# An attention and feed-forward kernel: another order of attention blocks, weights converted earlier through three raw buffers, and the activations' cast on ScalarE

## The chip, the cores and the metric

The kernel runs on one core of a Trainium2 chip. A core has five engines that work side by side, each through its own instructions in order: TensorE (PE in the profile; its weight loads are PEld) multiplies matrices, VectorE (DVE) and GpSimd (POOL) do elementwise work, ScalarE (ACT) does functions and copies, and SyncE (SP) issues most transfers. The metric is the device time of one execution in microseconds, the median of several.

## The reference

Attention over 2 batches of 8 heads, 768 positions and 64 numbers a head, where each query sees the first 8 keys and the 96 up to itself, then two feed-forward layers over the 1536 tokens, all in float32.

```python
scores = scale * np.matmul(q, k.transpose(0, 1, 3, 2))
is_global = pos[None, :] < int(n_global)            # 8
is_local = (rel >= 0) & (rel < int(n_local))        # 96
scores = scores + bias[None, :, :, :]               # -slope of the head * distance
scores = np.where(is_global | is_local, scores, -1000000000.0)
a = np.exp(scores - np.max(scores, axis=-1, keepdims=True))
x = np.matmul(a / (np.sum(a, axis=-1, keepdims=True) + 1e-09), v)   # then tokens x 512
h = x @ w_in                                        # 512 -> 2048
x = (np.maximum(h, 0.0) + np.log1p(np.exp(-np.abs(h)))) @ w_out     # 2048 -> 512
h = x @ w2_in
out = (h * np.clip(h + 3.0, 0.0, 6.0) / 6.0) @ w2_out
```

## The kernel before

**Attention.** The 1536 tokens are 12 blocks of 128, six for each batch, taken in the order 0 to 11. The heads of a block are taken in two quads of four, so there are 24 quads; quad k belongs to block k // 2. A quad has three steps: `s`, its scores (line 445), with a reduction on VectorE (L451), exponentials on ScalarE (L456), and VectorE's reciprocals (L341, L342) that GpSimd multiplies in (L344, tile `pm`); `t`, the transposes of the probabilities (L477, copied by ScalarE in L479 to `pT`); and `v`, the product with the values (L495, `px`). A block sees the slot of its own 128 keys and that of the block before. The first block of a batch has no block before: its two quads have one slot (128 keys) where others have two (256). I call them cheap quads below. `load_block` loads a block's `qT`, `kT` and `V` when the scores of the block ahead of it are taken.

**Feed-forward layers.** Each float32 matrix is split in a high and a low part, and each product is made of three matmuls (L179). A layer's 2048 hidden numbers are 16 chunks of 128. A weight *unit* is one chunk of `w_in` (u = 0) or `w_out` (u = 1), 512 KB of 64-bit words: `unit_load` issues its transfer on SP's queue into a buffer `raw` (two of them at that time), `unit_convert` makes the two parts: ScalarE takes the magnitude (L121), GpSimd clips it (L124), VectorE puts the bits together (L125, L128, L129), `cast` makes the high part (`w0`, `w2`; L98 on GpSimd while `in_first` holds, else L100 on ScalarE), and VectorE the low one (`w1`, `w3`; L134). `w3_1` is the low part of `w_out` of chunk 1, `wa` the work tile, and `raw3_1` the raw words of unit 1 of chunk 3. An activation `g` is computed by `split_g` and split into `gh` (a `cast`, like that of the weights) and `gl` (L171). Names with an f at the end (`ghf`, `accf`, `hf`) are those of the first phase.

**The program's order.** A lead of five steps (`LEAD`) takes the first quads; behind each step `LEAD_UNITS` says how many units are converted. Then `run` goes through 18 items: six groups of 256 tokens, each with three pairs of chunks. An item has two halves of 24 matmuls: h (`hf`, the products with `w_in`) and o (`accf`, those with `w_out`). They are interleaved as h0, h1, h2, o0, h3, o1, h4, o2 and so on. A half also carries one quad's `s` and `v` at its start and two transposes inside; behind it `HALF_UNITS` units are converted (one, where the table has ended). Attention ends with the items' first dozen; then its buffers are given to more weight slots and raw buffers (`grow`). When the 18 items are done, `in_first` falls, and 78 items with matmuls 512 wide follow, with little but matmuls on the path. A scheduler orders each engine's instructions from this program.

```python
            rest = between()
            for z, call in enumerate(calls):
                for f in rest.get(z, ()):
                    f()
                self.ordered(call)
            self.weight_step(HALF_UNITS[min(self.halves, len(HALF_UNITS) - 1)])
```

Of the kernel before, what the change touches and what calls it, by code (L numbers as in the profile page):

```python
# [29 lines left out]
H_AHEAD = 2  # L30
LEAD_UNITS = (0, 1, 1, 1, 1)
HALF_UNITS = (1, 1, 2, 1, 1, 1, 1)
WARM, FILL = 12, (6, 4, 2, 0, 0)
# [15 lines left out]
class Layers:  # L49
# [6 lines left out]
    def __init__(self, ctx, tc, weights, xsh, xsl, out):  # L56
        self.ctx, self.tc, self.nc = ctx, tc, tc.nc
        self.weights, self.xsh, self.xsl, self.out = weights, xsh, xsl, out
        self.pool("mp", 2)
# [10 lines left out]
        self.free, self.h_tags, self.acc_tags, self.wr = [], [], [], []  # L70
        self.n_h, self.halves, self.in_first = 0, 0, True
        self.grow(0, FIRST_SLOTS, 2, 2)
# [22 lines left out]
    def cast(self, out, in_):  # L95

        if self.in_first:
            self.nc.gpsimd.tensor_scalar(out=out, in0=in_, scalar1=1.0, scalar2=0.0, op0=ALU.mult, op1=ALU.add)  # L98
        else:
            self.nc.scalar.copy(out, in_)  # L100

    def unit_load(self, x):
        j, u = self.order[x]
        layer, f = divmod(j, NCH)
        raw = self.wr[x % len(self.wr)].tile([P, CW, 2], I32, tag="raw", name=f"raw{j}_{u}")
        self.nc.sync.dma_start(out=raw.rearrange("p c t -> p (c t)"), in_=self.weights[2 * layer + u][f])
        self.raws[x] = raw
# [28 lines left out]
    def weight_step(self, m):  # L136
        total = 4 * NCH
        for _ in range(m):
            x = self.done
            if x >= total or (self.order[x][1] == 0 and not self.free):  # L140
                return
            while self.loaded <= min(x + 2 * len(self.wr) - 1, total - 1):
                self.unit_load(self.loaded)
                self.loaded += 1
            self.unit_convert(x)
            self.done += 1

    def split_g(self, layer, hf, n):
# [6 lines left out]
        if layer == 0:  # L155
            t2 = self.tp.tile([P, 512], F32, tag="t", name=f"t2{n}")
            nc.scalar.activation(t1, hf, AF.Abs)  # L157
            nc.scalar.activation(t1, t1, AF.Exp, scale=-1.0)
            if self.in_first:
                nc.gpsimd.tensor_scalar(out=t2, in0=t1, scalar1=1.0, scalar2=1.0, op0=ALU.mult, op1=ALU.add)  # L160
            else:
                nc.scalar.add(t2, t1, 1.0)
            nc.scalar.activation(t3, t2, AF.Ln)
            nc.vector.scalar_tensor_tensor(out=t2, in0=t2, scalar=-1.0, in1=t1, op0=ALU.add, op1=ALU.subtract)  # L164
            nc.vector.scalar_tensor_tensor(out=t3, in0=hf, scalar=0.0, in1=t3, op0=ALU.max, op1=ALU.add)  # L165
            nc.vector.tensor_tensor(out=t3, in0=t3, in1=t2, op=ALU.subtract)
# [64 lines left out]
    def item(self, layer, ph, G, s):  # L231
# [17 lines left out]
        for m in range(4):  # L249
# [35 lines left out]
    def run(self, att=None, spare_step=lambda: None):  # L285
# [61 lines left out]
def fast_path(tc, ident, nf, q, k, qt, kt, v, weights, out, flag):  # L347


    with ExitStack() as ctx, ExitStack() as actx:  # L350
        nc = tc.nc
        xsh, xsl = x_tiles(ctx, tc)
        layers = Layers(ctx, tc, weights, xsh, xsl, out)
        tp = layers.tp
        ap2 = actx.enter_context(tc.tile_pool(name="ap2", bufs=2))
        ap_v = actx.enter_context(tc.tile_pool(name="ap_v", bufs=3))
# [5 lines left out]
        ps_x = actx.enter_context(tc.tile_pool(name="ps_x", bufs=1, space=PSUM))  # L362
        kT = ap1.tile([P, KC, 3, P], F32, name="kT")
        gk = ap1.tile([P, KC, MAX_GLOBAL], F32, name="gk")
        qT, V, px = {}, {}, {}
        zeros = ap1.tile([P, 512], BF16, name="zeros")
        nc.vector.memset(zeros, 0.0)

        def load_block(n):
            qT[n] = ap2.tile([P, KC, P], F32, tag="qT", name=f"qT{n}")  # L370
            V[n] = [ap_v.tile([P, DM], F32, tag="V", name=f"V{n}")]
            for cs in (slice(0, 1), slice(1, KC)) if n == 0 else (slice(0, KC),):
                nc.sync.dma_start(out=qT[n][:, cs], in_=qt[n][:, cs])
                nc.sync.dma_start(out=kT[:, cs, n % 3, :], in_=kt[n][:, cs])
# [391 lines left out]
```

## Time and profile before

| what | value |
|---|---|
| median of three runs | 686.46 us (685.08 to 688.02) |
| profiled execution | 685.12 us, its span 683.3 us |
| TensorE busy | 634.4 us (93% of the span), mean granted clock 0.972 |
| VectorE, ScalarE, GpSimd busy | 437.8, 357.2 and 166.4 us |

The span runs from the first to the last instruction that the profiler saw; what the execution takes beyond it (1.8 us) lies around it. [...] A busy share is a mean over stages: the stage with the attention and the first phase of the layers (up to about 235 us) looks unlike the one behind it.

### The profile page before, as it was taken

How to read it: one execution, taken by the hardware profiler on the slowest of the kernel's cores; microseconds unless marked ns; L12 is line 12 of the kernel's file. 1: busy time of each engine (PE TensorE's matmuls, PEld its weight loads, DVE VectorE, ACT ScalarE, POOL GpSimd, SP SyncE). 2: the span in 40 equal slices, each digit the busy share in tenths (PEclk: the TensorE clock that was granted, in tenths of full speed). 3: DMA queues.
4: the chain of work that ended last, by engine and by line, in shares of the span. 5: the costliest groups of instructions: out<-in, count | busy, mean ns of one | idle time of the engine just before them, and what ended most of it. 6: DMA issues, size and time to landing. Idle time of an engine off the chain costs nothing.

```text
span 683.3 us, 9612 instructions
## 1 busy us (share of the span) xinstructions
PE 634.4 (93%) x3481; PEld 522.1 (76%) x3481; DVE 437.8 (64%) x894; ACT 357.2 (52%) x749; POOL 166.4 (24%) x237
## 2 busy tenths in 40 slices
PE   8764876999997999999999999999999999999996
PEld 4553766888996988787888888888888788888884
DVE  6868345555399999999998999322752424324243
ACT  6945434776553477677677765233667222222221
POOL 4884433433255442234320021000100000000000
PEclk9988888999999999999999999999999999999998
DMA  7433323121023224142320123100265000001011
GB/s 231 143 113 116 109 66 116 39 67 55 33 93 124 94 92 147 70 154 93 123 94 31 62 64 121 63 0 1 78 197 157 1 1 0 1 0 62 0 63 66
DMA packets 24936, 53.66 MB, mean 79 GB/s; under 512 B 2480, under 2 KB 8880, under 8 KB 24880
## 3 DMA queue, kind: packets, MB, share of 16 engines
q1 hardware_dynamic: 24880, 52.96, 23.9%
q8 instruction: 29, 0.48, 0.3%
q14 instruction: 27, 0.22, 0.1%
HBM read 49.81 MB, written 3.15 MB: 77 GB/s over the span
## 4 chain that ended last, share of the span: by engine, by line
PE 65%; DVE 21%; ACT 5%; POOL 3%; issue 3%; DMA 1%; POOLq 0%; DVEq 0%; SPq 0%; ACTq 0%
PE acc L179 27%; PE h L179 26%; PE hf L179 4%; DVE wa L128 4%; PE accf L179 3%; DVE w L134 3%; DVE wa L129 3%; ACT pm L456 2%; POOL pm L344 2%; PE ptp L477 2%; PE s L445 2%; DVE wa L125 2%; PE px L495 1%; DVE pm L451 1%; DVE t2f L164 1%
## 5 line engine op out<-in xcount | busy, mean ns | idle before, releaser
L179 PE MATMUL h<-xsh,w 128*128 128x512 f32 x624 | 170.5, 396 | 1.9 <-DVE t3f L165 1.6
L179 PEld LDWEIGHTS h<-xsh,w 128*128 128x128 f32 x624 | 116.7, 188 | 30.6 <-DVE t3f L165 1.8
L179 PE MATMUL acc<-w,gh 128*128 128x512 f32 x384 | 120.6, 395 | 0.0
L124 POOL TENSOR_SCALAR wa<-wa 128x512 f32<-128x512 f32 x64 | 66.4, 1041 | 219.5 <-ACT wa L121 218.0
L169 DVE SCALAR_TENSOR_TENSOR t<-t,h 128x512 f32<-128x512 f32 x48 | 32.9, 686 | 98.2 <-ACT t L168 98.1
L168 ACT ACTIVATE t<-h,three 128x512 f32<-128x512 f32 x48 | 33.0, 687 | 107.2 <-PE h L179 107.0
L179 PE MATMUL h<-xsl,w 128*128 128x512 f32 x312 | 86.7, 395 | 0.0
L179 PE MATMUL accf<-ghf,w 128*128 128x256 f32 x288 | 66.8, 312 | 20.5 <-DVE w L134 20.4
L179 PEld LDWEIGHTS acc<-w,gh 128*128 128x128 f32 x384 | 72.0, 188 | 17.5
L171 DVE TENSOR_TENSOR gl<-t,gh 128x512 fp32r<-128x512 f32 x78 | 55.4, 710 | 46.3 <-ACT gh L100 46.1
L179 PE MATMUL acc<-gh,w 128*128 128x512 f32 x240 | 78.2, 396 | 1.3 <-DVE part L264 1.3
L100 ACT CAST gh<-t 128x512 fp32r<-128x512 f32 x78 | 48.3, 619 | 58.2 <-PE acc L179 25.6
L179 PE MATMUL acc<-w,gl 128*128 128x512 f32 x192 | 76.1, 396 | 0.1
L179 PEld LDWEIGHTS accf<-ghf,w 128*128 128x128 f32 x288 | 52.5, 211 | 23.2 <-DVE w L134 21.7
L179 PEld LDWEIGHTS h<-xsl,w 128*128 128x128 f32 x312 | 58.5, 188 | 14.0
L344 POOL TENSOR_SCALAR pm<-pm,rs 128x256 f32<-128x256 f32 (+1 forms) x96 | 52.5, 565 | 46.9 <-DVE rs L342 35.1
L134 DVE TENSOR_TENSOR w<-wa,w 128x512 fp32r<-128x512 f32 x64 | 46.5, 730 | 16.2 <-POOL w L98 8.9
L179 PEld LDWEIGHTS acc<-gh,w 128*128 128x128 f32 x240 | 45.1, 188 | 12.9 <-ACT t L157 1.7
L121 ACT ACTIVATE wa<-raw 128x512 f32<-128x512 f32 x64 | 42.5, 673 | 22.8 <-DVE w L134 14.4
L456 ACT ACTIVATE pm<-pm,nm 128x256 f32<-128x256 f32 (+1 forms) x96 | 46.2, 484 | 14.8 <-DVE nm L451 14.7
L179 PE MATMUL hf<-xsh,w 128*128 128x256 f32 x288 | 45.7, 290 | 7.9 <-DVE w L134 7.9
L451 DVE CUSTOM_DVE_ANT_0 pm<-s,bias 128x256 f32<-128x256 f32 (+1 forms) x96 | 33.4, 397 | 28.9 <-PE s L445 27.2
(90 smaller groups left out, 1008.3 us busy)
## 6 DMA issues: line engine op xcount, KB each, us to landing
raw<-in_w1i SPq DMA_DIRECT2D x16, 512.0 KB, 3.3
raw<-in_w1o SPq DMA_DIRECT2D x16, 512.0 KB, 3.3
raw<-in_w2i SPq DMA_DIRECT2D x16, 512.0 KB, 3.2
raw<-in_w2o SPq DMA_DIRECT2D x16, 512.0 KB, 3.3
V<-in_v SPq DMA_DIRECT2D x12, 256.0 KB, 2.9
chk<-in_q SPq DMA_DIRECT2D x12, 256.0 KB, 3.4
chk<-in_k SPq DMA_DIRECT2D x12, 256.0 KB, 2.8
out_x<-part SPq DMA_DIRECT2D x12, 256.0 KB, 2.1
```

The costliest lines, as they stand in the source:

```text
L100: self.nc.scalar.copy(out, in_)
L121: first = nc.scalar.activation(a, raw.bitcast(F32)[:, :, 1], AF.Abs)
L124: nc.gpsimd.tensor_scalar(out=a, in0=a, scalar1=W_HI, scalar2=W_LO, op0=ALU.min, op1=ALU.max)
L128: nc.vector.scalar_tensor_tensor(out=ai, in0=hi, scalar=-2 ** 30, in1=ai, op0=ALU.bitwise_and, op1=ALU.bitwise_or)
L134: nc.vector.tensor_tensor(out=wl, in0=a, in1=r32(wh), op=ALU.subtract)
L168: nc.scalar.activation(t1, hf, AF.Relu, bias=self.three[:, 0:1])
L169: nc.vector.scalar_tensor_tensor(out=t3, in0=t1, scalar=6.0, in1=hf, op0=ALU.min, op1=ALU.mult)
L171: nc.vector.tensor_tensor(out=gl, in0=t3, in1=r32(gh), op=ALU.subtract)
L179: return self.nc.tensor.matmul(out, lhsT=a, rhs=b, start=start and z == 0, stop=stop and z == len(seq) - 1, **kw)
L344: nc.gpsimd.tensor_scalar(out=t, in0=t, scalar1=rs[:, j:j + 1], scalar2=0.0, op0=ALU.mult, op1=ALU.add)
L451: nc.vector.tensor_tensor_reduce(out=pmz, in0=ps[z % 2][:, z // 2, 0:nsl, :].rearrange("p s t -> p (s t)"), in1=bias[:, 4 * e + z, mo:mo + ...
L456: nc.scalar.activation(pmz, pmz, AF.Exp, bias=nm[:, z:z + 1], scale=-1.0, accum_out=sm[:, z:z + 1])
```

## The change

The blocks are taken as 0, 6, 1 to 5, 7 to 11, so that all four cheap quads come first; `kT` gets a fourth slot and `V` a tile of its own for block 6, which block 7 still needs, and the rows of the output are numbered by `ORDER`. `LEAD_UNITS` converts six units in the lead in place of four, and `HALF_UNITS` two behind the first half. A third raw buffer (`more_raw`) exists as long as attention does. The activations' cast `gh` is always ScalarE's. A new flag `beside`, which falls when attention ends, takes the place of `in_first` for the addition `t2` and the weights' cast, so these leave GpSimd earlier.

```diff
-LEAD_UNITS = (0, 1, 1, 1, 1)
-HALF_UNITS = (1, 1, 2, 1, 1, 1, 1)
+LEAD_UNITS = (0, 1, 1, 2, 2)
+HALF_UNITS = (2, 1, 1, 1, 1)
+RAW_BUFS = 3
...
+ORDER = [0, NB, *range(1, NB), *range(NB + 1, 2 * NB)]
...
     def cast(self, out, in_):
 
-        if self.in_first:
+        if self.beside:
             self.nc.gpsimd.tensor_scalar(out=out, in0=in_, scalar1=1.0, scalar2=0.0, op0=ALU.mult, op1=ALU.add)
         else:
             self.nc.scalar.copy(out, in_)
...
-        raw = self.wr[x % len(self.wr)].tile([P, CW, 2], I32, tag="raw", name=f"raw{j}_{u}")
+        pools = self.wr + self.more_raw if x < 2 * PHASES[0][0] else self.wr
+        raw = pools[x % len(pools)].tile([P, CW, 2], I32, tag="raw", name=f"raw{j}_{u}")
...
-            while self.loaded <= min(x + 2 * len(self.wr) - 1, total - 1):
+            ahead = 2 * len(self.wr + self.more_raw)
+            if self.beside:
+                ahead = min(ahead, max(2 * PHASES[0][0] - x, 2))
+            while self.loaded <= min(x + ahead - 1, total - 1):
                 self.unit_load(self.loaded)
...
-            if self.in_first:
+            if self.beside:
                 nc.gpsimd.tensor_scalar(out=t2, in0=t1, scalar1=1.0, scalar2=1.0, op0=ALU.mult, op1=ALU.add)
...
-        self.cast(gh, t3)
+        nc.scalar.copy(gh, t3)
         nc.vector.tensor_tensor(out=gl, in0=t3, in1=r32(gh), op=ALU.subtract)
...
-                t0 = G * GB + m * P
+                t0 = self.rows[G * GB // P + m] * P
...
                     att.close()
+                    self.beside, self.more_raw = False, []
                 self.grow(1, MORE_SLOTS, 2, 2)
...
+        layers.beside, layers.rows = True, ORDER
         tp = layers.tp
+        layers.more_raw = [actx.enter_context(tc.tile_pool(name="ap_r", bufs=RAW_BUFS - 2))]
...
-        kT = ap1.tile([P, KC, 3, P], F32, name="kT")
-        gk = ap1.tile([P, KC, MAX_GLOBAL], F32, name="gk")
+        kT = ap1.tile([P, KC, 4, P], F32, name="kT")
+        gk = [ap1.tile([P, KC, MAX_GLOBAL], F32, name=f"gk{b}") for b in range(B)]
...
+        def slot_of(n):
+
+            return 3 if n == NB else (n - n // NB) % 3
+
...
-            V[n] = [ap_v.tile([P, DM], F32, tag="V", name=f"V{n}")]
+            V[n] = [ap1.tile([P, DM], F32, name="V_kept") if n == NB else ap_v.tile([P, DM], F32, tag="V", name=f"V{n}")]
...
-            n, e = divmod(k, KC // 2)
-            i, slot = n % NB, n % 3
+            z, e = divmod(k, KC // 2)
+            n = ORDER[z]
+            i, slot, first = n % NB, slot_of(n), gk[n // NB]
             if e == 0:
-                if n + 1 < B * NB:
-                    load_block(n + 1)
+                if z + 1 < B * NB:
+                    load_block(ORDER[z + 1])
...
-            g, o = divmod(n * P, GB)
+            g, o = divmod(z * P, GB)
```

What this does to the engines' order is seen at three places.

On GpSimd, around the quad that follows the lead and three halves (`pm10`, its scores are taken in o0). Line numbers of the changed kernel are higher (L98 becomes L101, L124 L128, L344 L352). Before:

```order
L160 TENSOR_SCALAR t2f2_851<-t1f2_849 128x512
L98 TENSOR_SCALAR w2_0_341<-wa0_1_829 128x512
L344 TENSOR_SCALAR pm10_870<-pm10_870,rs10_885 128x256 x4
L98 TENSOR_SCALAR w2_1_406<-wa1_1_839 128x512
L98 TENSOR_SCALAR ghf2_847<-t3f2_850 128x512
L124 TENSOR_SCALAR wa2_1_943<-wa2_1_943 128x512
L98 TENSOR_SCALAR w2_2_468<-wa2_1_943 128x512
```

Changed:

```order
L101 TENSOR_SCALAR w2_0_349<-wa0_1_640 128x512
L167 TENSOR_SCALAR t2f2_860<-t1f2_858 128x512
L101 TENSOR_SCALAR w2_1_410<-wa1_1_650 128x512
L128 TENSOR_SCALAR wa2_1_753<-wa2_1_753 128x512
L352 TENSOR_SCALAR pm10_879<-pm10_879,rs10_894 128x256 x4
L128 TENSOR_SCALAR wa3_1_848<-wa3_1_848 128x512
L101 TENSOR_SCALAR w2_2_464<-wa2_1_753 128x512
```

The high part `w2_1` moved from behind pm10's four scalings to ahead of them, and the cast `ghf2` left the engine. On ScalarE that cast now stands between the copies of transposed probabilities of one half and the exponentials (L471) of the next:

```order
L494 COPY pT8_0_919<-ptp8_0_918 128x512
L494 COPY pT8_1_938<-ptp8_1_937 128x512
L125 ACTIVATE wa4_1_950<-raw4_1_648 128x512
L177 CAST ghf2_856<-t3f2_859 128x512
L471 ACTIVATE pm11_961,sm11_963<-pm11_961,nm11_962 128x256 x4
L494 COPY pT9_0_1000<-ptp9_0_999 128x512
L494 COPY pT9_1_1019<-ptp9_1_1018 128x512
```

Three magnitudes (`wa2_1`, `wa3_1`, `wa4_1`; two of them just above these rows) are now ahead of pm11's exponentials; before, `wa3_1` was behind them.

On VectorE, the second unit that o1 needs (`w3_3`). Before, behind the reductions of quad 12 (L451), whose scores are taken at the start of o1:

```order
L451 ISA pm12_1055,nm12_1056<-s12_1_1054,bias_145 128x128
L451 ISA nm12_1056 128x1
L125 TENSOR_SCALAR wa3_1_1025<-wa3_1_1025 128x512
L341 TENSOR_SCALAR rs12_1070<-sm12_1057 128x4
L128 SCALAR_TENSOR_TENSOR wa3_1_1025<-raw3_1_941,wa3_1_1025 128x512
L342 RECIPROCAL rs12_1070<-rs12_1070 128x4
L503 TENSOR_TENSOR xsl1_81<-px4_976,xsh1_78 128x4x128
L129 SCALAR_TENSOR_TENSOR wa3_1_1025<-raw3_1_941,wa3_1_1025 128x512
L164 SCALAR_TENSOR_TENSOR t2f3_1037<-t2f3_1037,t1f3_1035 128x512
L165 SCALAR_TENSOR_TENSOR t3f3_1036<-hf10_4_951,t3f3_1036 128x512
L134 TENSOR_TENSOR w3_3_537<-wa3_1_1025,w2_3_536 128x512
L166 TENSOR_TENSOR t3f3_1036<-t3f3_1036,t2f3_1037 128x512
```

Changed (L134 becomes L138, L451 L466, L171 L178):

```order
L129 TENSOR_SCALAR wa3_1_848<-wa3_1_848 128x512
L132 SCALAR_TENSOR_TENSOR wa3_1_848<-raw3_1_638,wa3_1_848 128x512
L138 TENSOR_TENSOR w3_2_465<-wa2_1_753,w2_2_464 128x512
L133 SCALAR_TENSOR_TENSOR wa3_1_848<-raw3_1_638,wa3_1_848 128x512
L178 TENSOR_TENSOR glf2_857<-t3f2_859,ghf2_856 128x512
L138 TENSOR_TENSOR w3_3_479<-wa3_1_848,w2_3_478 128x512
L466 ISA pm11_961,nm11_962<-s11_0_959,bias_149 128x256
L466 ISA nm11_962 128x1
L466 ISA pm11_961,nm11_962<-s11_0_959,bias_149 128x256
```

It moved to ahead of the reductions of quad 11, whose scores are taken at the start of h3, the half before o1.

On SP's queue, the transfers behind those of the first two blocks. Before:

```order
L374 DMA kT_130<-in_kt 128x4x128
L375 DMA V2_247<-in_v 128x512
L106 DMA raw0_0_335<-in_w1i 128x1024
L106 DMA raw1_0_337<-in_w1i 128x1024
L373 DMA qT2_246<-in_qt 128x512
L373 DMA qT3_351<-in_qt 128x512
L374 DMA kT_130<-in_kt 128x4x128
L373 DMA qT4_478<-in_qt 128x512
L374 DMA kT_130<-in_kt 128x4x128
```

Changed:

```order
L388 DMA kT_133<-in_kt 128x4x128
L389 DMA V1_251<-in_v 128x512
L110 DMA raw0_0_339<-in_w1i 128x1024
L110 DMA raw1_0_341<-in_w1i 128x1024
L110 DMA raw2_0_343<-in_w1i 128x1024
L388 DMA kT_133<-in_kt 128x4x128
L389 DMA V2_360<-in_v 128x512
L387 DMA qT1_250<-in_qt 128x512
L387 DMA qT2_359<-in_qt 128x512
```

A third weight load, and a `kT` and a `V` load, moved to ahead of `qT1`, the queries of the third block to be taken (in the order before, that is qT2, row 5 of the first list).

## Rows read from the trace of the kernel before

**Rows 1.** Stretches: from:to, length, busy us of PE PEld DVE ACT POOL, PEclk, DMA share, GB/s

```profile
30.80:115.30 84.50, 56.10 (x424) 49.60 (x422) 51.54 (x143) 40.18 (x109) 44.63 (x66) 0.82 0.34 110
115.30:182.00 66.70, 64.41 (x597) 56.87 (x596) 33.32 (x123) 44.07 (x119) 23.38 (x47) 1.00 0.19 56
182.00:235.00 53.00, 48.40 (x380) 47.22 (x377) 48.94 (x68) 23.09 (x39) 27.12 (x33) 0.97 0.29 99
235.00:310.00 75.00, 73.47 (x337) 59.34 (x336) 73.92 (x120) 55.64 (x96) 23.90 (x23) 1.00 0.33 114
```

**Rows 2.** TensorE's waits, 0 to 182 us: us in total, times, longest

```profile
PE accf L179 <- DVE w L134: 20.4, 4, 5.9
PE hf L179 <- DVE w L134: 7.9, 3, 5.2
```

**Rows 3.** TensorE's timeline, 30 to 130 us: start, us, work [idle before it <-releaser]

```profile
45.08 1.23 PE L179 MATMUL hf<-xsh,w 128*128 128x256 f32 x4 [5.20 <-DVE w L134]
...
55.95 0.74 PE L179 MATMUL hf<-xsh,w 128*128 128x256 f32 x4 [1.99 <-DVE w L134]
...
64.57 0.58 PE L179 MATMUL accf<-ghf,w 128*128 128x256 f32 x1 [4.41 <-DVE w L134]
...
70.59 0.58 PE L179 MATMUL accf<-ghf,w 128*128 128x256 f32 x1 [5.02 <-DVE w L134]
...
76.03 1.13 PE L445 MATMUL s<-kT,qT 64*128 64x256 f32 x8
...
90.20 0.58 PE L179 MATMUL accf<-ghf,w 128*128 128x256 f32 x1 [5.88 <-DVE w L134]
...
109.64 0.58 PE L179 MATMUL accf<-ghf,w 128*128 128x256 f32 x1 [5.12 <-DVE w L134]
...
115.27 1.34 PE L445 MATMUL s<-kT,qT 64*128 64x256 f32 x8
```

**Rows 4.** The chain that ended last, from 100 to 145 us: start, us, what

```profile
116.61 0.59 PE px L495 x8
...
127.34 1.06 PE s L445 x8
128.41 1.02 PE px L495 x16
...
140.00 1.06 PE s L445 x8
```

**Rows 5.** GpSimd's timeline, 62 to 80 us

```profile
66.60 2.62 POOL L344 TENSOR_SCALAR pm<-pm,rs 128x256 f32<-128x256 f32 x4 [3.03 <-DVE rs L342]
69.19 0.62 POOL L98 TENSOR_SCALAR w<-wa 128x512 fp32r<-128x512 f32 x1
76.19 0.62 POOL L98 TENSOR_SCALAR ghf<-t3f 128x512 fp32r<-128x512 f32 x1 [6.38 <-PE accf L179]
```

**Rows 6.** VectorE's timeline, 62 to 72 us

```profile
69.85 0.69 DVE L134 TENSOR_TENSOR w<-wa,w 128x512 fp32r<-128x512 f32 x1 [2.26 <-POOL w L98]
```

**Rows 7.** GpSimd's groups, 30 to 235 us: xcount | busy, mean ns | idle before

```profile
L98 POOL TENSOR_SCALAR ghf<-t3f 128x512 fp32r<-128x512 f32 x16 | 11.1, 693 | 30.9 <-PE accf L179 19.7 <-DVE t3f L166 11.1
```

**Rows 8.** ScalarE's groups by line, 235 to 420 us

```profile
L100 ACT CAST gh<-t 128x512 fp32r<-128x512 f32 x32 | 19.8, 618 | 17.4 <-DVE t L166 10.0 <-PE acc L179 6.2 <-PE h L179 1.2
```

**Rows 9.** One stretch in the lead, columns as in rows 1

```profile
8.00:12.00 4.00, 3.34 (x20) 2.18 (x22) 1.87 (x17) 3.35 (x18) 1.87 (x6) 1.00 1.06 384
```

**Rows 10.** TensorE's timeline in the lead

```profile
15.01 1.13 PE L445 MATMUL s<-kT,qT 64*128 64x256 f32 x8
```

**Rows 11.** VectorE's groups by line, 182 to 232 us

```profile
L171 DVE TENSOR_TENSOR glf<-t3f,ghf 128x512 fp32r<-128x512 f32 x6 | 5.6, 938 | 0.8 <-POOL ghf L98 0.8
```

**Rows 12.** VectorE's groups by line, 232 to 310 us

```profile
L171 DVE TENSOR_TENSOR gl<-t,gh 128x512 fp32r<-128x512 f32 x11 | 8.0, 728 | 0.0
```

**Rows 13.** TensorE's waits, 182 to 310 us

```profile
PE accf L179 <- DVE glf L171: 3.0, 1, 3.0
PE h L179 <- DVE t3f L165: 1.6, 1, 1.6
```

More of the change, by code (lines that the diff above doesn't have):

```diff
@@ L58, in __init__ @@
         self.weights, self.xsh, self.xsl, self.out = weights, xsh, xsl, out
+        self.rows = range(T // P)
         self.pool("mp", 2)
@@ L69, in __init__ @@
         self.order += [(j, u) for j in range(len(first), 2 * NCH) for u in range(2)]
-        self.free, self.h_tags, self.acc_tags, self.wr = [], [], [], []
-        self.n_h, self.halves, self.in_first = 0, 0, True
+        self.free, self.h_tags, self.acc_tags, self.wr, self.more_raw = [], [], [], [], []
+        self.n_h, self.halves, self.in_first, self.beside = 0, 0, True, False
         self.grow(0, FIRST_SLOTS, 2, 2)
@@ L367, in fast_path @@
         nc.vector.memset(zeros, 0.0)
+        def slot_of(n):
+            return 3 if n == NB else (n - n // NB) % 3
         def load_block(n):
             qT[n] = ap2.tile([P, KC, P], F32, tag="qT", name=f"qT{n}")
-            V[n] = [ap_v.tile([P, DM], F32, tag="V", name=f"V{n}")]
+            V[n] = [ap1.tile([P, DM], F32, name="V_kept") if n == NB else ap_v.tile([P, DM], F32, tag="V", name=f"V{n}")]
             for cs in (slice(0, 1), slice(1, KC)) if n == 0 else (slice(0, KC),):
                 nc.sync.dma_start(out=qT[n][:, cs], in_=qt[n][:, cs])
-                nc.sync.dma_start(out=kT[:, cs, n % 3, :], in_=kt[n][:, cs])
+                nc.sync.dma_start(out=kT[:, cs, slot_of(n), :], in_=kt[n][:, cs])
             nc.sync.dma_start(out=V[n][0], in_=v[n * P:(n + 1) * P, :])
@@ L421, in att_s @@
         def att_s(k):
-            n, e = divmod(k, KC // 2)
-            i, slot = n % NB, n % 3
+            z, e = divmod(k, KC // 2)
+            n = ORDER[z]
+            i, slot, first = n % NB, slot_of(n), gk[n // NB]
             if e == 0:
-                if n + 1 < B * NB:
-                    load_block(n + 1)
+                if z + 1 < B * NB:
+                    load_block(ORDER[z + 1])
                 if i == 0:
-                    nc.vector.tensor_copy(gk, kT[:, :, slot, 0:MAX_GLOBAL])
-            before = (n - 1) % 3
+                    nc.vector.tensor_copy(first, kT[:, :, slot, 0:MAX_GLOBAL])
+            before = slot_of(n - 1) if i else slot + 1
             w = P if i == 0 else 2 * P
@@ L435, in att_s @@
             end = slot + nsl * step
-            ks = slice(slot, min(end, 3) if end >= 0 else None, step)
+            ks = slice(slot, min(end, 4) if end >= 0 else None, step)
             two = layers.acc_tags if k < LEAD and k % 2 else s_tags
@@ L459, in att_s @@
             if e == KC // 2 - 1 and 1 <= i < NB - 1:
-                nc.vector.tensor_copy(kT[:, :, slot, 0:MAX_GLOBAL], gk)
+                nc.vector.tensor_copy(kT[:, :, slot, 0:MAX_GLOBAL], first)
             pms[k] = pm
         def att_t(k, a):
-            n, e = divmod(k, KC // 2)
-            nsl = 1 if n % NB == 0 else 2
+            z, e = divmod(k, KC // 2)
+            nsl = 1 if ORDER[z] % NB == 0 else 2
             pm = pms[k] if a == 0 else pms.pop(k)
@@ L482, in att_v @@
         def att_v(k):
-            n, e = divmod(k, KC // 2)
+            z, e = divmod(k, KC // 2)
+            n = ORDER[z]
             i = n % NB
```

## The prediction

> **What bounds the kernel now.** I read the page first: TensorE is busy for 93% of the span, so time can only come from the places where it idles or runs at the lower clock. The table of stretches shows where those are [rows 1]. [...] After 182 little is open: 4.6 us idle up to 235, 1.5 us up to 310.
>
> TensorE's waits up to 182 us have one cause: VectorE's last step of a weight unit, `w` [rows 2]. Products into `accf` wait four times for 20.4 us, products into `hf` three times for 7.9 us. TensorE's timeline places them [rows 3]: 5.20 us before 45.08 (in h1), 1.99 before 55.95 (h2), 4.41 and 5.02 in o0, 5.88 in o1 (before 90.20) and 5.12 in o2 (before 109.64). o0 ends where the next quad's scores start, at 76.03; o2 ends at 115.27. In the steady part two halves take 140.00 − 127.34 = 12.66 us in the chain that ended last [rows 4], so 6.33 each. Between 76.03 and 115.27 lie four halves (h3, o1, h4, o2) in 39.24 us, where four at 6.33 would be 25.3. The 13.9 us too much are the two waits (11.0) and 2.9 us of lower clock around them.
>
> **The change, part by part.**
>
> *Units earlier.* Now the unit that o1 needs in its second half of products is converted on VectorE after pm12's reductions, so within o1 itself. In the changed order `w3_2` and `w3_3` stand ahead of pm11, whose scores are computed in h3, a half before o1; `w3_5` stands ahead of pm13, so it is done during o1 for use in o2. Each therefore has about 6.33 us more, and the waits were 5.88 and 5.12 us. What stands in the way on VectorE is four instructions a unit, 0.5 to 0.7 us each, as that of 0.69 us [rows 6]; VectorE has 33.32 us of work in 66.70 in the steady part, so it has room. I take both waits and their lower clock as gone: **−13.9**. The bounds are 0 (the unit gets later by as much as it is asked for earlier) and −13.9.
>
> *The opening, up to the end of o0.* Here I walk wait by wait.
> - The third raw buffer puts one more weight load, and a kT and a V load, ahead of qT1 on SP's queue: 512 KB and twice 256 KB, 1.0 MB. The DMA engines are full at 8 to 12 us and move 384 GB/s [rows 9], so this is 2.7 us of transfer, partly behind scores that start only at 15.01 [rows 10]. Estimate **+0.5** at h1 (0 to 2.7).
> - h1's 5.20 stays: its unit has the same place on VectorE.
> - h2's 1.99 goes, since six units instead of four are converted before the first half: **−1.9**.
> - o0's first wait, 4.41: `w3_0` still comes after pm10's reductions on VectorE; only the conversions of the opening around it thin out. **−1.1** (0 to −4.4).
> - o0's second wait, 5.02: now `w2_1` is cast on GpSimd after pm10's four scalings, which wait 3.03 us for VectorE and then take 2.62 [rows 5]; only then VectorE makes the low part, at 69.85 after 2.26 us of waiting [rows 6]. In the changed order `w2_1` stands ahead of those scalings. That frees at most 3.03 + 2.62 us of GpSimd's queue; VectorE's own work before `w3_1` stays. I take **−3.1** (0 to −5.0).
> - A shorter second wait leaves less of what follows it at the lower clock: **−0.9**, a third of the 2.9 above, for one wait out of four that shrinks.
>
> Sum of the opening: 0.5 − 1.9 − 1.1 − 3.1 − 0.9 = **−6.5**.
>
> *Block order.* The values of a cheap quad (one slot of keys) take 0.59 us on TensorE and of a full one 1.02 [rows 4]. The two cheap quads of the second batch ran inside the halves and now run in the lead, where TensorE has gaps; their places go to full quads: 2 × 0.43, and an estimated 0.4 for the transposes: **+1.3**. Work in the lead falls by as much, behind transfers [rows 9], so I count no gain there.
>
> *Casts on ScalarE.* GpSimd's cast of the activations took 693 ns each, 16 of them [rows 7]; ScalarE's takes 618 [rows 8]. While attention lasts, ScalarE is busy for 44.07 of 66.70 us [rows 1] and gets 11 such casts in some 150 us, 6.8 us: hidden by that room. Without this room each costs 0.6. After attention it also gets the casts of weights and the additions `t2f`, 27 instructions of about 0.62 us, 17 us, beside its 23.09 of 53.00: still below TensorE.
>
> *After attention.* VectorE is busy for 48.94 of 53.00 us from 182 to 235, and its L171 takes 938 ns beside GpSimd's work against 728 later [rows 11, 12]. TensorE's two main waits there are for such VectorE steps, 3.0 and 1.6 us [rows 13]. With 27 instructions less on GpSimd I take the 4.6 us of idle time as nearly gone: **−4.5**. Bounds: 0, and −7.7 with the 1.5 us up to 310 and the clock's 0.03 of 53 (1.6).
>
> [...]
>
> **Sum.** −13.9 − 6.5 + 1.3 − 4.5 = −23.6. The profiled execution took 685.1 us (span 683.3), which gives 661.5; the median of the runs is 1.3 above it, so **663 us**.
>
> **The rivals.**
> - *B, the opening's waits go too.* If loads and conversions in the lead get far enough ahead, all eight halves from 30.8 on run at 6.33: 50.6 instead of 84.5 us, −33.9, and with +1.3 and −4.5 649 us. For it: six units in the lead. Against: `w3_0` stays behind pm10, and VectorE is busy for 51.54 of 84.50 us already. 648 to 657, point 652.
> - *C, only the later half gains.* The extra 1.0 MB delays the scores, hence the softmax and with it the conversions, and the opening's gain is eaten; VectorE stays the bound after attention. −13.9 + 1.3 to −13.9 + 1.3 + 2 gives 673 to 676; with part of the rest, 671 to 678.
> - *D, nothing is gained.* The units are asked for earlier, but raw buffers come free only as conversions end, so conversion simply starts at the old time. Then +1.3 for the blocks and noise, 683 to 690. Against: the changed order puts the conversions ahead of a half's reductions, whatever the buffers do.
> - *E, slower.* The cast of the activations needs a buffer that TensorE releases at the end of an o half: on GpSimd that wait was 19.7 us in all [rows 7], 6.38 us of it before 76.19 [rows 5]. On ScalarE the exponentials and the copies of transposed probabilities of the next half are queued behind it, and TensorE waits for the copies. At 2 us for each of 16 casts this is +32, so 685.1 + 32 − 23.6 + 1.3 = 695. It decides from 23.6/16 = 1.5 us a cast. Against: GpSimd's long waits were the shadow of TensorE's own stalls. The cast stands behind its half's copies, ahead of exponentials whose scores TensorE computes in about 1.1 us after the same release; a cast of 0.62 fits in.
>
> [...]
>
> **How the numbers follow.** A (the sum, 657 to 670) 0.55; B 0.18; C 0.15; D 0.06; E 0.06. The time is A's. From 649 to 678 lie A, C and nearly all of B, and about 0.14 is left out. A measurement of this kernel can tell about 0.5% (3.4 us) from no change. A, B and C are faster by more: 0.88; D is the same: 0.06; E is slower: 0.06.
>
> **What would show it.** In the changed trace: four halves after o0 in 25 to 26 us, with no wait for `w` (else D or C); o0's end at about 69.5 instead of 76.03, with h1's 5 us still there (B: none; C: 76 or later); a granted clock near 1.00 after o0; ScalarE's casts of activations with no long wait that ends in a TensorE wait for pT (E); L171 near 730 ns and TensorE's idle time under 1 us between the end of attention and 50 us later. [...]

## The result and the profile after

The changed kernel takes **664.2 us** (663.94 to 666.43, four runs) where the one before takes 685.77 (684.88 to 688.02): a ratio of 0.9688, 95% interval 0.9655 to 0.9721. The forecast was 663, between 649 and 678. The profiled execution took 664.26 us, its span 662.4 (before 683.3), so 20.9 us are to be placed.

The table of stretches, as [rows 1] (columns as there):

```profile
30.80:115.30 84.50, 66.61 (x562) 57.63 (x560) 64.04 (x178) 53.74 (x140) 48.81 (x72) 0.92 0.36 115
115.30:182.00 66.70, 65.47 (x602) 59.87 (x599) 34.56 (x108) 46.48 (x114) 17.19 (x35) 1.00 0.16 52
182.00:235.00 53.00, 53.00 (x372) 49.42 (x372) 49.87 (x83) 44.20 (x79) 13.01 (x14) 1.00 0.32 110
```

From 30.8 to 115.3 us TensorE now does 66.61 us of work where it did 56.10, at a granted clock (PEclk, TensorE's clock as a share of full speed) of 0.92 where it was 0.82. From 182 to 235 it is busy without a gap, 53.00 of 53.00, where it was busy for 48.40. What [rows 13] showed there is gone: no wait of TensorE is left between 160 and 300 us. ScalarE has 44.20 us of work there in place of 23.09, GpSimd 13.01 in place of 27.12.

TensorE's waits up to 182 us, as [rows 2]:

```profile
PE hf L186 <- DVE w L138: 8.5, 5, 4.4
PE accf L186 <- DVE w L138: 5.9, 2, 4.3
PE ptp L492 <- ACT pT L494: 4.7, 7, 1.9
```

The products into `accf` wait for 5.9 us in place of 20.4, two times in place of four; those into `hf` wait as long as before (8.5, was 7.9); and transposes now wait for ScalarE's copies (`pT`) for 4.7 us.

TensorE's timeline, as [rows 3]:

```profile
35.01 0.74 PE L186 MATMUL hf<-xsh,w 128*128 128x256 f32 x4 [2.09 <-DVE w L138]
...
40.20 0.74 PE L186 MATMUL hf<-xsh,w 128*128 128x256 f32 x4 [0.97 <-DVE w L138]
...
46.70 1.22 PE L186 MATMUL hf<-xsh,w 128*128 128x256 f32 x4 [4.37 <-DVE w L138]
...
58.46 1.13 PE L460 MATMUL s<-kT,qT 64*128 64x256 f32 x8
...
64.88 0.44 PE L186 MATMUL accf<-ghf,w 128*128 128x256 f32 x1 [4.26 <-DVE w L138]
...
67.42 0.58 PE L186 MATMUL accf<-ghf,w 128*128 128x256 f32 x1 [1.67 <-DVE w L138]
...
73.01 1.13 PE L460 MATMUL s<-kT,qT 64*128 64x256 f32 x8
...
79.81 0.66 PE L492 MATMUL ptp<-ident,pm 128*128 128x128 f32 x4 [1.89 <-ACT pT L494]
...
92.82 0.63 PE L492 MATMUL ptp<-ident,pm 128*128 128x128 f32 x4 [0.78 <-ACT pT L494]
...
100.68 1.13 PE L460 MATMUL s<-kT,qT 64*128 64x256 f32 x8
```

The waits in o1 (5.88) and o2 (5.12) have no row any more. In o0 the second wait fell from 5.02 to 1.67 and the first stayed (4.26, was 4.41). h1's stayed too (0.97 and 4.37, was 5.20), and h0 has one of 2.09, where it had 0.70. New are 1.89 in h3 and 0.78 in h4, for `pT`.

The marks of these timelines cut the span into four pieces: up to the end of o0, the four halves up to the end of o2, from there to the start of the last product with the values (181.08 before, 166.97 after), and the rest of the span. I use the same cuts for every kernel below.

| piece, us | before | after | moved | forecast |
|---|---|---|---|---|
| to the end of o0 | 76.03 | 73.01 | −3.0 | −6.5 |
| h3, o1, h4, o2 | 39.24 | 27.67 | −11.6 | −13.9 |
| to the last product with values | 65.81 | 66.29 | +0.5 | +1.3 |
| rest | 502.22 | 495.43 | −6.8 | −4.5 |

### The profile page after: what moved, and what is told of

The parts are those of the page before. It is cut to its first block, busy times and chain, and to the rows that moved or that the text cites. A ratio compares the mean times of both kernels' runs of the same rounds, so it can differ in the third digit from the quotient of the medians.

```text
span 662.4 us, 9594 instructions
## 1 busy us (share of the span) xinstructions
PE 630.1 (95%) x3480; PEld 517.8 (78%) x3481; DVE 430.1 (65%) x894; ACT 375.7 (57%) x786; POOL 145.9 (22%) x200
## 4 chain that ended last, share of the span: by engine, by line
PE 68%; DVE 19%; ACT 5%; POOL 3%; issue 2%; DMA 1%; SPq 0%; POOLq 0%; ACTq 0%; DVEq 0%
PE h L186 26%; PE acc L186 25%; PE hf L186 6%; PE accf L186 5%; DVE wa L132 3%; ACT pm L471 3%; DVE w L138 3%; DVE wa L133 2%; PE s L460 2%; POOL pm L352 2%; PE ptp L492 2%; DVE pm L466 2%; DVE wa L129 1%; DVE t L172 1%; DVE t L171 1%
## 5 line engine op out<-in xcount | busy, mean ns | idle before, releaser
L128 POOL TENSOR_SCALAR wa<-wa 128x512 f32<-128x512 f32 x64 | 72.4, 1135 | 252.5 <-ACT wa L125 250.6
L178 DVE TENSOR_TENSOR gl<-t,gh 128x512 fp32r<-128x512 f32 x78 | 54.3, 696 | 43.6 <-ACT gh L177 43.4
L186 PE MATMUL accf<-ghf,w 128*128 128x256 f32 x288 | 60.9, 295 | 5.9 <-DVE w L138 5.9
L352 POOL TENSOR_SCALAR pm<-pm,rs 128x256 f32<-128x256 f32 (+1 forms) x96 | 52.3, 562 | 53.9 <-DVE rs L350 21.2
L471 ACT ACTIVATE pm<-pm,nm 128x256 f32<-128x256 f32 (+1 forms) x96 | 46.2, 482 | 14.8 <-DVE nm L466 13.9
L186 PEld LDWEIGHTS accf<-ghf,w 128*128 128x128 f32 x288 | 48.0, 194 | 8.0 <-DVE w L138 6.5
L138 DVE TENSOR_TENSOR w<-wa,w 128x512 fp32r<-128x512 f32 x64 | 45.8, 717 | 12.5 <-ACT w L103 8.2
L132 DVE SCALAR_TENSOR_TENSOR wa<-raw,wa 128x512 int32<-128x512 int32 x64 | 47.6, 745 | 0.4
```

Of the source, the lines that this page charges most:

```text
L128: nc.gpsimd.tensor_scalar(out=a, in0=a, scalar1=W_HI, scalar2=W_LO, op0=ALU.min, op1=ALU.max)
L132: nc.vector.scalar_tensor_tensor(out=ai, in0=hi, scalar=-2 ** 30, in1=ai, op0=ALU.bitwise_and, op1=ALU.bitwise_or)
L138: nc.vector.tensor_tensor(out=wl, in0=a, in1=r32(wh), op=ALU.subtract)
L186: return self.nc.tensor.matmul(out, lhsT=a, rhs=b, start=start and z == 0, stop=stop and z == len(seq) - 1, **kw)
L352: nc.gpsimd.tensor_scalar(out=t, in0=t, scalar1=rs[:, j:j + 1], scalar2=0.0, op0=ALU.mult, op1=ALU.add)
L471: nc.scalar.activation(pmz, pmz, AF.Exp, bias=nm[:, z:z + 1], scale=-1.0, accum_out=sm[:, z:z + 1])
```

## The experiments

Twelve kernels ran, in three groups of four; each group has its own runs of the kernel before on its chip (medians 687.55, 686.72 and 686.71 us), so kernels of different groups are compared by their ratios to it. Each edit is against the changed kernel, except where the text says the kernel before. The pieces are those of one profiled execution each. Runs of one kernel differ by up to 4.5 us (e11: 659.87 to 664.38), so a piece that is one or two microseconds shorter shows something only where the medians agree with it.

| kernel | median us | ratio to before, interval | to end of o0 | four halves | to last product | rest |
|---|---|---|---|---|---|---|
| changed | 664.2 | 0.9688 (0.9655 to 0.9721) | 73.01 | 27.67 | 66.29 | 495.4 |
| e1, activations' cast on GpSimd | 663.6 | 0.9659 (0.9636 to 0.9681) | 73.49 | 26.37 | 66.49 | 495.5 |
| e2, old block order | 661.8 | 0.9635 (0.9613 to 0.9658) | 73.29 | 23.97 | 65.88 | 495.2 |
| e3, old unit tables | 682.3 | 0.9930 (0.9906 to 0.9953) | 80.45 | 37.74 | 66.31 | 496.2 |
| e4, two raw buffers | 664.0 | 0.9660 (0.9635 to 0.9685) | 73.13 | 27.36 | 66.29 | 496.1 |
| e5, GpSimd to the end of the phase | 668.0 | 0.9727 (0.9693 to 0.9761) | 72.48 | 27.57 | 66.37 | 499.6 |
| e8, before + tables | 668.6 | 0.9727 (0.9684 to 0.9770) | 72.75 | 26.19 | 65.63 | 501.7 |
| e9, before + tables + flag | 660.7 | 0.9615 (0.9581 to 0.9650) | 73.73 | 25.84 | 65.62 | 495.7 |
| e10, e9 + weights' cast on ScalarE | 661.2 | 0.9621 (0.9584 to 0.9657) | 76.10 | 24.26 | 65.62 | 495.4 |
| e11, e9 + a seventh unit in the lead | 661.1 | 0.9638 (0.9614 to 0.9662) | 70.84 | 26.12 | 65.64 | 495.8 |
| f1, block 6 at place 3 | 659.5 | 0.9605 (0.9592 to 0.9618) | 69.89 | 26.41 | 66.44 | 495.8 |
| f2, block 6 at place 5 | 663.3 | 0.9662 (0.9644 to 0.9680) | 74.13 | 24.40 | 66.35 | 495.9 |
| f4, old order + a seventh unit | 662.9 | 0.9661 (0.9646 to 0.9677) | 75.26 | 24.65 | 65.87 | 495.9 |

### One part undone at a time

**e1.** The activations' cast back where it was, as long as attention lasts.

```diff
-        nc.scalar.copy(gh, t3)
+        self.cast(gh, t3)
```

> The changed kernel (664.2 us) with the activations' cast back on GpSimd while attention lasts; all else as changed. Theory A (the gain of the four halves after o0 comes from asking for the units earlier): about 664 to 667, the waits for w in o1 and o2 stay away, and the wait for pT in h3 (1.89 us) shrinks. Theory B (it comes from taking the cast off GpSimd, where the cast waits for TensorE and holds the weights' casts queued behind it): 671 to 676, with waits of 4 us and more for w back in o1 and o2.

TensorE's timeline, the scores at the end of o0 and of o2:

```profile
73.49 1.13 PE L460 MATMUL s<-kT,qT 64*128 64x256 f32 x8
...
99.86 1.13 PE L460 MATMUL s<-kT,qT 64*128 64x256 f32 x8
```

663.6 us: the cast's place gives nothing. The waits for `w` in o1 and o2 stay away. The 1.89 us wait in h3 is gone and the four halves are 1.3 us shorter (26.37), while the opening is 0.5 longer; the times cannot be told apart. Theory B falls.

**e2.** The old order.

```diff
-ORDER = [0, NB, *range(1, NB), *range(NB + 1, 2 * NB)]
+ORDER = list(range(2 * NB))
```

> The changed kernel with the blocks in the old order 0 to 11 (the fourth slot of kT and the kept V stay). Theory A (the order only moves work of TensorE from the halves to the lead or back): 663 to 665. Theory C (the cheap quads in the lead leave VectorE and GpSimd free for the conversions of the opening): the opening to the end of o0 takes 3 us and more longer, 667 to 672.

TensorE's timeline, the scores that start each of the four halves (x8 of 64x128 are those of a cheap quad), and the two waits for `pT` inside them:

```profile
73.29 1.13 PE L460 MATMUL s<-kT,qT 64*128 64x256 f32 x8
...
78.71 0.66 PE L492 MATMUL ptp<-ident,pm 128*128 128x128 f32 x4 [0.50 <-ACT pT L494]
...
80.02 0.71 PE L460 MATMUL s<-kT,qT 64*128 64x128 f32 x8
...
85.59 0.71 PE L460 MATMUL s<-kT,qT 64*128 64x128 f32 x8
...
91.17 1.13 PE L460 MATMUL s<-kT,qT 64*128 64x256 f32 x8
...
96.19 0.44 PE L492 MATMUL ptp<-ident,pm 128*128 128x128 f32 x2 [0.33 <-ACT pT L494]
...
97.26 1.14 PE L460 MATMUL s<-kT,qT 64*128 64x256 f32 x8
```

Neither theory: by the medians the kernel came out faster than theory A said, 661.8 us. Against the changed kernel itself the two ratios' intervals touch (0.9655 and 0.9658). But in e2's own group all four of its runs (660.14 to 662.30) lie below all runs of e1 and e4 (662.89 to 664.80), two kernels that keep the new order and whose times cannot be told from the changed kernel's. So the new order costs about 2 us.

In the profiles the opening ends at the same time (73.29), and the four halves take 23.97 us where they took 27.67. About 1.3 of these 3.7 us is TensorE's own work: the scores of two cheap quads (0.71 us each, 1.13 for a full quad) and the transposes of one. Another 2.3 are waits for `pT`, 0.50 and 0.33 us here, 1.89, 0.78 and 0.41 in the changed kernel. The largest of them falls in h3, ahead of the first cheap quad, so it isn't the cheap quads' smaller work in these halves that takes it away. What does was not tried apart.

**e3.** The old tables of units.

```diff
-LEAD_UNITS = (0, 1, 1, 2, 2)
-HALF_UNITS = (2, 1, 1, 1, 1)
+LEAD_UNITS = (0, 1, 1, 1, 1)
+HALF_UNITS = (1, 1, 2, 1, 1, 1, 1)
```

> The changed kernel with the old tables LEAD_UNITS and HALF_UNITS. Theory A: the waits for w in o1 and o2, 5 us each with the lower clock behind them, come back, 672 to 677. Theory B (the cast on ScalarE alone does it) or the third buffer alone: at most 2 us more, 664 to 666.

TensorE's waits up to 182 us:

```profile
PE accf L186 <- DVE w L138: 18.8, 4, 5.4
PE hf L186 <- DVE w L138: 9.2, 3, 3.9
```

682.3 us, worse than theory A said: the waits for `w` are nearly those of [rows 2], four for 18.8 us. The two pieces in which the tables act take 80.45 and 37.74 us, 7.4 and 10.1 more than in the changed kernel.

**e4.** No third raw buffer.

```diff
-        layers.more_raw = [actx.enter_context(tc.tile_pool(name="ap_r", bufs=RAW_BUFS - 2))]
```

> The changed kernel without the third raw buffer. Theory A1 (the early conversions need the third buffer): units come later, waits for w in h1, o0 or o1 grow, 667 to 672. Theory A2 (the third buffer only puts a transfer ahead of the queries of the third block): the wait in h0 falls from 2.09 to under 1 us and the halves start as early or earlier, 662 to 664.

664.0 us, every piece as with three, and h0 waits 2.09 us as it did. Both theories fall: the buffer neither helps the conversions nor holds up the queries of the third block. VectorE's copy `gk` of block 6's first keys, of which the section on the prediction speaks, waits here as in the changed kernel:

```profile
9.37 0.23 DVE L443 COPY gk<-kT 128x128 f32<-128x128 f32 x1 [2.76 <-DMA kT<-in_kt]
```

**e5.** The addition and the weights' cast stay on GpSimd until the first phase ends.

```diff
-                    self.beside, self.more_raw = False, []
+                    self.more_raw = []
...
-        self.in_first = False
+        self.in_first = self.beside = False
```

> The changed kernel with the addition t2 and the weights' cast left on GpSimd up to the end of the first phase, as in the kernel before (the activations' cast stays on ScalarE). Theory A (GpSimd's work beside VectorE's costs TensorE what the stretch after attention gained, 7 us between the end of attention and the end of the span): 669 to 672, with TensorE's waits for VectorE after 182 us back. Rival F (taking the activations' cast off GpSimd is enough there): 664 to 666.

The stretch after attention:

```profile
182.00:235.00 53.00, 50.39 (x351) 46.70 (x350) 52.56 (x76) 31.37 (x55) 23.05 (x29) 0.97 0.29 100
```

668.0 us, a little under theory A's range: more than half of TensorE's gap (2.61 us, 4.60 in the kernel before) and its clock of 0.97 are back, and the last piece takes 499.6 us in place of 495.4. So 4.2 us of the 6.8 come with these two operations. The flag also limits how many units are loaded ahead, and this limit now lasts longer, too; but TensorE's waits from 160 to 310 us are for activations (`t3f` 1.9, `glf` 0.8 us), and none is for a weight. Rival F falls, but some is right in it: with the activations' cast on GpSimd too (e8, further down) that piece takes 501.7, another 2.1.

### One or two parts alone

**e8.** The kernel before with the two new tables and nothing else.

> The kernel before with the new tables LEAD_UNITS and HALF_UNITS alone: two raw buffers, old block order, all casts on GpSimd. Theory A (the tables are the gain, as undoing them in the changed kernel cost 18 us): 668 to 674. Rival G (they need the casts on ScalarE or the new order to take effect): 678 to 686, with the waits for w in o1 and o2 still there.

TensorE's waits up to 182 us:

```profile
PE ptp L477 <- ACT pT L479: 9.2, 10, 2.2
...
PE accf L179 <- DVE w L134: 1.5, 1, 1.5
```

668.6 us: by themselves the tables take 2.7% off. Of the four waits of products into `accf` one is left, 1.5 us, while transposes now wait 9.2 us in all for ScalarE's copies (2.3 in the kernel before). Theory A holds, rival G falls.

**e9.** The tables, and a flag that takes all casts and `t2` off GpSimd when attention ends.

```diff
...
                     att.close()
+                    self.beside = False
...
```

> The kernel before with the new tables and, when attention ends, all casts and t2 off GpSimd; no new block order, no third raw buffer, the activations' cast on GpSimd beside attention. Theory A (these two parts are the whole gain, the other three give nothing): 660 to 665. Rival G (the other three are needed): 668 and more.

The stretch after attention:

```profile
182.00:235.00 53.00, 53.00 (x365) 49.06 (x365) 51.21 (x86) 44.87 (x80) 13.46 (x14) 1.00 0.34 113
```

660.7 us, and its interval (0.9581 to 0.9650) lies just below that of the changed kernel (0.9655 to 0.9721): the two parts are the whole gain. The other three together bring nothing. By the ratios they cost 0.7%, or 0.45% if e1 and e4 stand for the changed kernel, whose intervals overlap e9's. From e8 to e9 only the flag differs, and the last piece falls from 501.7 to 495.7 us.

**e10.** From e9, the opening's weights' cast moved as well.

```diff
-        self.cast(wh, a)
+        nc.scalar.copy(wh, a)
```

> As e9_tables_and_flag, and the weights' cast is on ScalarE from the start. Theory H (what is left in the opening comes from the casts queued behind the scalings of the probabilities on GpSimd): the waits for w in h1 and o0 shrink by 3 us and more, 655 to 660. Rival I (ScalarE's exponentials and copies are held up by as much, or VectorE's own work is the limit): 661 to 667, with longer waits for pT or for VectorE's reductions.

TensorE's timeline in o0:

```profile
70.98 0.58 PE L179 MATMUL accf<-ghf,w 128*128 128x256 f32 x1 [8.22 <-DVE w L134]
```

661.2 us. h1's wait did not shrink (5.26 against 4.83 in e9) and o0's became one of 8.22. Theory H falls. Rival I named the time. Of its two reasons one is not seen, since TensorE's transposes wait less for `pT` (3.4 us up to 182, 8.8 in e9). The other, VectorE's own work, fits: the cast that o0 waits for starts on ScalarE only at 68.49, after 2.26 us in which ScalarE waits for VectorE's bits of the same unit. The unit is late ahead of its cast.

### Where the cheap quads stand, and one unit more

**f1 and f2.** The second cheap block at place 3 or at place 5 of the changed kernel's order.

```diff
-ORDER = [0, NB, *range(1, NB), *range(NB + 1, 2 * NB)]
+ORDER = [0, 1, 2, NB, *range(3, NB), *range(NB + 1, 2 * NB)]
...
+ORDER = [*range(5), NB, 5, *range(NB + 1, 2 * NB)]
```

> The changed kernel with block 6 (the second cheap one) at place 3 of the order, so that quads 6 and 7 are cheap; all else as changed. Theory K (a cheap quad is worth most where conversions crowd GpSimd and VectorE): pm6's and pm7's scalings, 5.03 us in a row on GpSimd before the cast of w0_2, halve, o0 ends 2 us and more before 73.0, the four halves behind it take about the 27.7 us of the changed kernel; 660 to 663. Rival L (in the halves it is only worth TensorE's own time, about 1 us, wherever it stands): 663 to 665.

> The changed kernel with block 6 at place 5, so that quads 10 and 11 are cheap (scores in o0 and h3). Theory K: the four halves behind o0 take 24 to 26 us as with the old order (23.97) and o0 itself is a little shorter; 660 to 662. Rival L: 663 to 665.

GpSimd's timeline behind the start of the first half, first of the changed kernel, then of f1:

```profile
33.80 5.03 POOL L352 TENSOR_SCALAR pm<-pm,rs 128x256 f32<-128x256 f32 x8
38.80 0.62 POOL L101 TENSOR_SCALAR w<-wa 128x512 fp32r<-128x512 f32 x1
```

```profile
32.32 1.50 POOL L352 TENSOR_SCALAR pm<-pm,rs 128x128 f32<-128x128 f32 x3
...
34.50 2.59 POOL L352 TENSOR_SCALAR pm<-pm,rs 128x128 f32<-128x128 f32 x4
...
37.65 0.37 POOL L352 TENSOR_SCALAR pm<-pm,rs 128x128 f32<-128x128 f32 x1
38.10 0.62 POOL L101 TENSOR_SCALAR w<-wa 128x512 fp32r<-128x512 f32 x1
```

VectorE's timeline of the changed kernel, behind that cast:

```profile
39.45 0.69 DVE L138 TENSOR_TENSOR w<-wa,w 128x512 fp32r<-128x512 f32 x1 [3.69 <-POOL w L101]
```

TensorE's timeline of f1:

```profile
40.66 0.74 PE L186 MATMUL hf<-xsh,w 128*128 128x256 f32 x4 [2.48 <-DVE w L138]
...
43.84 1.22 PE L186 MATMUL hf<-xsh,w 128*128 128x256 f32 x4 [0.66 <-DVE w L138]
...
51.56 0.93 PE L186 MATMUL hf<-xsh,w 128*128 128x256 f32 x4 [2.04 <-DVE w L138]
...
56.87 0.75 PE L186 MATMUL hf<-xsh,w 128*128 128x256 f32 x4 [2.25 <-DVE w L138]
...
58.71 1.14 PE L460 MATMUL s<-kT,qT 64*128 64x256 f32 x8
...
62.19 0.38 PE L186 MATMUL accf<-ghf,w 128*128 128x256 f32 x1 [1.75 <-DVE w L138]
...
64.77 0.39 PE L186 MATMUL accf<-ghf,w 128*128 128x256 f32 x1 [1.96 <-DVE w L138]
...
69.89 1.13 PE L460 MATMUL s<-kT,qT 64*128 64x256 f32 x8
...
96.30 1.13 PE L460 MATMUL s<-kT,qT 64*128 64x256 f32 x8
```

In the changed kernel eight scalings of full quads (5.03 us) stand in a row ahead of a weights' cast, and VectorE idles 3.69 us for that cast; in f1 eight of a cheap block take 1.50 + 2.59 + 0.37 us, not half as theory K said, with conversions between them. h1's waits fall from 0.97 and 4.37 us to 2.48 and 0.66, and h0's is gone, but h2 has two of 2.04 and 2.25 in place of 1.05 in all. So o0 starts no earlier than in the changed kernel (58.71, there 58.46). The opening's gain comes within o0: it waits 1.75 and 1.96 us, there 4.26 and 1.67, and ends at 69.89.

The place of the one cheap block is the only difference between f1 and f2, in one group, and it is worth 3.9 us (659.5 and 663.3, with intervals that do not touch). f1 also beats the changed kernel (its interval ends at 0.9618). f2 has the short four halves that theory K said (24.40), but o0 ends 1.1 us later than in the changed kernel and the time, 663.3, is rival L's. So the place matters, as theory K said, and f1's time lies just below its range. That the scalings in h0 and h1 are what does it is not shown, since their gain was waited away again in h2.

**f4 and e11.** Seven units in the lead, with the changed kernel's other parts in the old order, and on e9.

```diff
-LEAD_UNITS = (0, 1, 1, 2, 2)
+LEAD_UNITS = (0, 1, 2, 2, 2)
```

> The changed kernel with the old block order and seven units converted in the lead in place of six. Theory H2 (the waits for w in h1 and o0 come from conversions that start late): they shrink by 2 us and more in all, 657 to 660. Rival I2 (VectorE and GpSimd are full up to o0, and what is converted earlier only moves the wait into the lead): the halves start later by what the waits lose, 661 to 664.

> The kernel before with the flag that frees GpSimd after attention, the new tables, and seven units converted in the lead in place of six; old order, two raw buffers, the activations' cast on GpSimd beside attention. Theory H2: 656 to 659. Rival I2: 660 to 663, as without the seventh unit (660.7).

662.9 and 661.1 us, no better than e2 and e9. H2 falls twice: the seventh unit takes no wait away. h1's is 4.83 us in e11 as in e9, and in f4 there are 4.20 in h2 (1.49 in e2) and 5.40 in o0 (5.59). That e11's opening ends at 70.84 (e9's at 73.73) comes from its first half, which starts at 30.67 in the profiled execution and at 34.05 in e9's. The medians do not show it. The times are those of rival I2, but a later start of the halves, which it gave as the reason, is not seen.

## Why the prediction was right, step by step

**Units earlier** was the gain, as forecast, and a little mis-sized. The 13.9 us had both waits and the lower clock; all of that went (o1 and o2 had a granted clock of 0.76 and 0.77, and all four halves now have 1.00), and e8 and e3 show from both sides that the tables did it. Missing are 2.3 us, the waits for `pT` in h3 and h4. The rows show how the first came about, ScalarE's timeline in h3:

```profile
74.48 0.61 ACT L177 CAST ghf<-t3f 128x512 fp32r<-128x512 f32 x1
77.21 0.51 ACT L471 ACTIVATE pm<-pm,nm 128x256 f32<-128x256 f32 x1 [2.12 <-DVE nm L466]
...
79.19 0.56 ACT L494 COPY pT<-ptp 128x512 f32<-128x512 f32 x1
```

and VectorE's, with two rows of the lead ahead of them:

```profile
9.33 0.23 DVE L444 COPY gk<-kT 128x128 f32<-128x128 f32 x1 [2.65 <-DMA kT<-in_kt]
9.48 0.28 DVE L466 CUSTOM_DVE_ANT_0 pm<-s,bias 128x128 f32<-128x128 f32 x1
...
75.12 0.69 DVE L178 TENSOR_TENSOR glf<-t3f,ghf 128x512 fp32r<-128x512 f32 x1 [0.66 <-ACT ghf L177]
75.73 1.10 DVE L138 TENSOR_TENSOR w<-wa,w 128x512 fp32r<-128x512 f32 x1
```

`ghf2` needs the buffer that TensorE releases at the end of o0 (73.01); behind it on VectorE stand `glf2` and `w3_3`, and only then quad 11's reductions, so ScalarE's exponentials start at 77.21 after 2.12 us of waiting, and the copy `pT` that TensorE needs is behind them, at 79.19. This is rival E's mechanism, at one place instead of sixteen: 1.89 us. It takes more than the cast: with the same cast on ScalarE, e2 waits 0.50 us in h3. The 0.78 in h4 is not shown to be the cast's, since e1, which has it on GpSimd, waits 0.78 us as well, in o1. E went wrong in taking a price for each cast. In the steady part the copy's wait is 0.41 us in every second half, where it was 0.46 to 0.47 before, and e1 shows that the whole place of the cast is worth less than can be measured.

**The opening** was forecast to gain too much: −6.5, and −3.0 came. The second wait in o0 shrank as worked out (by 3.35 us, forecast 3.1), and in sum no more than that came: o0 started at 58.46, before at 58.00. The step that failed is the sum of small terms around it. h2's waits fell by 0.9 and not 1.9, and o0's first by 0.15 and not 1.1. The lower clock, put at −0.9, gave nothing back: from the end of o0's first wait to the end of o0 the granted clock was 0.56 before (64.57 to 76.03) and 0.58 after (64.88 to 73.01). The windows of o0, before and after, have columns as in [rows 1]:

```profile
58.00:76.03 18.03, 8.60 (x57) 7.56 (x56) 9.05 (x22) 6.39 (x17) 7.27 (x13) 0.72 0.23 77
58.46:73.01 14.55, 8.62 (x58) 7.58 (x57) 13.03 (x28) 7.30 (x18) 11.99 (x15) 0.77 0.40 131
```

TensorE is busy for 8.62 us in o0, before for 8.60. And h0's wait, which is not in the sum, grew from the 0.7 us that remain of the 7.9 in [rows 2] to 2.09. This one goes with the block order: it is 2.09 to 2.12 us in the five kernels that have the new order (the changed one, e1, e3, e4, e5) and at most 0.9 in all others.

One cause was wrong as well. I had put a delay down to the third buffer's transfer, and e4 shows that it has none. Scores that I had at 15.01 [rows 10] did start later, at 17.81. In the two upper VectorE rows the copy `gk` for block 6 waits 2.65 us for its keys' transfer, and the first reductions, 7.32 before, stand behind it at 9.48; e4 has that row without the third buffer. But e9, which has neither the order nor the buffer, has these scores at 17.50 as well, and the first half's products start at 30.79 in the changed kernel, as they did before, so this late start was not what the opening lost. What sets h1's 4 to 5 us is open. f1 shows one delay ahead of it, GpSimd's scalings in front of a cast that VectorE awaits, and that this can be moved; neither a buffer nor a seventh unit nor ScalarE took h1's wait away.

**Block order** was priced by TensorE's own time, +1.3, and on the piece behind o2 +0.5 came. The price left out the scores, 0.42 us for each of the two quads by e2's rows. It was also counted in the wrong piece: the 25.3 us for four halves hold full quads only, so a part of it was in the −13.9 already, as e2's 23.97 us show. And more than TensorE's own work was at stake: with the new order the four halves also wait 2.3 us more for `pT`, and h0 waits 2.09 us. The step that failed is the price by TensorE's own time alone. That the lead brings no gain held in the end: the first half's products start at 30.79 with the new order and at 32.46 without (e2), but h0's wait takes that back, and o0 ends at 73.01 and 73.29.

**After attention** was mis-sized the other way, −4.5 against −6.8, near the bound of −7.7. L171 (L178 now) takes 681 ns where it took 938 [rows 11], as VectorE's groups from 182 to 232 us show:

```profile
L178 DVE TENSOR_TENSOR glf<-t3f,ghf 128x512 fp32r<-128x512 f32 x6 | 4.1, 681 | 0.0
```

With the two operations back on GpSimd (e5) VectorE is busy for 52.56 us of the 53.00 from 182 to 235 with 76 instructions, here for 49.87 with 83, and GpSimd for 23.05 in place of 13.01. So VectorE took longer for fewer instructions where GpSimd had more work; why it did is not shown. From the start of the last product with the values on, TensorE now idles 7.80 us where it idled 12.77, and is busy for 487.63 where it was for 489.45, at a clock of 1.00 in place of 0.99. So 5.0 of the 6.8 us are idle time and 1.8 busy time. I had taken the idle time up to 235 us alone, without the clock and the stretch behind it.

**The whole.** The errors were +3.5, +2.3, −0.8 and −2.3 us; they cancel to 2.7, so the profiled execution came out at 664.26 where 661.5 was forecast. The median is 1 us from the forecast because the 1.3 us that I added for the median above the profiled execution did not recur. That the time fits so closely is luck; that the tables are the main gain and the flag the second is shown. The rivals B (all waits of the opening gone), C and D did not happen.

## What to carry to other kernels

Where an engine waits for a conversion, ask first when it is asked for: here two tables of numbers, without a buffer, an order or an engine changed, took 2.7% off, and freeing GpSimd after attention, where VectorE was busy for 51.79 of 53.00 us (e8), another 1% (e9). Work that is cheap on the waiting engine is not cheap or dear by that engine's time alone (e2: 1.3 of the 3.7 us by which the four halves shrank were TensorE's own work). Try it at more than one place: one block's place was worth 3.9 us (f1 and f2), though f1's interval overlaps those of e2 and e9, so a best place is not shown. A change of five parts that gains should be taken apart all the same: of these five, two did nothing that the times show (e1, e4), and one, the order, cost about 0.3% (e2).

## What was not expected of the hardware

A copy of 0.23 us at the head of VectorE's queue held VectorE up for 2.65 us, because its operand was still being transferred (the row at 9.33 above), with reductions behind it that needed nothing of it. The first half's products started no later for it (30.79 us). And a kernel with its waits elsewhere can take the same time: e10's one wait of 8.22 us in o0 stands against shorter halves behind it (24.26 us, in e9 25.84), and the two medians are 661.2 and 660.7. Why the four halves got shorter there was not tried apart.
